# Recurrence kernel: the state's update issued ahead of VectorE's diagonal, the scatters one step later

## The chip, the cores and the metric

The kernel runs on one core of a Trainium2 chip. The metric is the device time of one execution in microseconds (us), from runs on the chip. All rows below are from one profiled execution.

## The reference

Three layers in a row on float32 data: a linear recurrence over 768 steps of time (4 batches, 8 heads, width 48), a layer of 8 experts in which each token goes to its best one, and a layer of 8 experts with 4 slots each that all tokens share. The change touches the first:

```
state = 0
for t in range(S):
    cur = u * k[t] (outer) v[t]
    y[t] = r[t] @ (state + cur)
    state = w * state + k[t] (outer) v[t]
```

The second layer takes y as rows x of 3072 tokens by 384: a token is computed if `x @ w_skip > 0`, and goes to the expert with the largest `x @ w_gate`. The third mixes all rows by two softmaxes.

## The kernel before

Time is cut into 6 chunks of 128; a chunk of one batch is one step of the loop at line 973, so 24 steps, step i with chunk `c = i // 4` and batch `b = i % 4`. Within a chunk the recurrence is done by matrix products: all pairs of times in the chunk give scores, which a mask and the powers of w weigh; the state carries what came before the chunk.

The order of the work is written out by hand: `manual_schedule` keeps every engine in the order in which the code emits its instructions, and waits between engines come from the buffers that the instructions read and write. What a step i emits, with its names:

- `load(i + 3)` (line 498): SyncE fetches r and k (`rkb`, two transfers) and k, v by rows (`kvt`), three steps ahead, with five buffers of each.
- `scores(i)` (626): TensorE makes the scores `sc` (line 633, two banks of PSUM, one buffer) from the scaled `rks`, and `dt` (636) from `pd`; ScalarE copies `dt` to `dts` (638).
- `inter(i - 1)` (694), `stateb(i - 1)` (670) and `trx(i - 2)` (717): the state's part of y, the copy of the state for it, and the turn of y into rows of x.
- `bonus(i)` (651): TensorE turns `dts` into the front columns of the tile `ud` (line 656), one bank of PSUM, of which there is one buffer. It holds the u term for the scores' diagonal.
- `prep(i + 1)` and `prepk(i + 1)` (611, 620): VectorE scales the next inputs to `rks` (616); GpSimd makes `pd` (618) and `kt` (624), which the next step's update needs.
- `amask(i)` (683): VectorE masks the scores into `at` (line 681) and puts the diagonal into them (688), read from the front columns of `ud`.
- `upd(i)` (640): TensorE makes the chunk's contribution to the state, eight products (line 649), into columns 160 to 351 of the same `ud`. Steps 20 to 23 have none.
- `state(i)` (658): GpSimd decays the old state to `tmp` (667), VectorE adds `ud` to it (668).
- `av(i - 1)` (704): TensorE's products of `at` and v into `yp` (712), copied out by ScalarE (715).

Every fourth step also routes the chunk before, in groups of four batches: `route1` (TensorE, 744) in one step; `route2` (TensorE, 804) and `route2b` (VectorE, 820 to 837) in the next; two steps on `route3` (TensorE, 847 to 856, into further columns of `ud`), `gates`, `places` and `count` (VectorE, 861 to 888, which also write the indices `idx`) and `route4` (GpSimd 903, ScalarE 905 and 907). With the indices there, `scat(j)` (890) has GpSimd write the rows of x of step j to their experts' slots by an indirect transfer (891): from step 8 on one in each step, the rest after the loop. In steps 8, 11 and 14 `wload` (912) fetches expert weights.

The dependencies are kept by bank of PSUM: two instructions of different engines that touch the same bank are put in the order of the code, even where their columns differ.

Of the kernel before, what the change touches and what calls it, by code (L numbers as in the profile page):

```python
# [461 lines left out]
def tile_main(ctx, tc, rk, kv, wu, wcat, phi, w1, w2, v1, v2, r_in, k_in, v_in, w_in, u_in, wcn, out, dbg=None, force=False):  # L462
# [177 lines left out]
    def upd(j):  # L640
        t = T[j]
        if j < NT - B:
            kt, kvt = t["kt"], t["kv"]
            up = t["up"] = t["ud"][0:PR, 160:352].rearrange("d (p e) -> d p e", p=4)
            for p in range(4):
                for hf in range(2):
                    h = 2 * p + hf
                    m = 64 if hf == 0 else D
                    nc.tensor.matmul(up[64 * hf : 64 * hf + m, p, :], kt[:, h * D : h * D + m], kvt[:, 1, h * D : h * D + D], start=True, stop=True)  # L649
# [28 lines left out]
    def past(j):  # L678
        t = T[j]
        at = t["at"] = wk.tile([P, 2, 4, P], F32, tag="at", name=f"at{j}")  # L680
        nc.vector.tensor_mul(at, t["sc"], mask.rearrange("s (a o t) -> s a o t", a=1, o=1).to_broadcast([P, 2, 4, P]))  # L681

    def amask(j):
        t = T[j]
        if "at" not in t:
            past(j)
        at = t["at"]
        nc.vector.copy_predicated(  # L688
            at,
            ident_i.rearrange("s (a o t) -> s a o t", a=1, o=1).to_broadcast([P, 2, 4, P]),  # L690
            t["dtk"].rearrange("s (p o r) -> s r p o", o=1, r=32)[:, 0:2].to_broadcast([P, 2, 4, P]),
        )
# [279 lines left out]
    if True:  # L972
        for i in range(NT):
            if i + 3 < NT:
                load(i + 3)
            rc, rb = divmod(i - 5, B)
            rok = 0 <= rc < NC_ - 1
            if i == 0:
                prep(0)
                for hf in range(2):  # L980
                    r0 = 64 * hf
                    nc.vector.tensor_copy(usel[r0 : r0 + D, :, hf : hf + 1], wt[r0 : r0 + D, 1, :].rearrange("p (a o) -> p a o", o=1))
            scores(i)
            if i > 0:
                inter(i - 1)
                stateb(i - 1)
            if i > 1:
                trx(i - 2)
            bonus(i)
            if i == 0:  # L990
                decays()
                warm(ps, "y", 7)
                prep(1)
                prepk(0)
                prepk(1)
                for b in range(B):
                    nc.gpsimd.memset(sbd[b], 0.0)
            elif i + 1 < NT:
                prep(i + 1)
                prepk(i + 1)  # L1000
            if rok and rb == 1:
                route2(rc)
            if rok and (rb == 3 or i == 23):
                route3(rc, place=T[i]["dk"][:, P:])
            if i == 22:
                mrt = rows(nc, cn, "t", rt, pa, "u", mcs[:, 0:1])
                nc.vector.tensor_copy(lx[:, 0:1, :], mrt)
            amask(i)
            upd(i)
            state(i)  # L1010
            if i > 0:
                av(i - 1)
            if rok and rb == 0:
                route1(rc)
            if i == 23:
                route1(5)
            if rok and rb == 1:
                route2b(rc)
            if i == 23:
                weave("gpgpgp", g=gates(4), p=places(4))  # L1020
            if rok and rb == 3:
                weave("gpgpgp", g=gates(rc), p=places(rc))
                count(rc)
                route4(rc)
            if i == 21:
                nc.vector.tensor_reduce(cmax, ltm[:, 0:16, :].rearrange("t b s -> t s b"), axis=AX.X, op=ALU.max)
                colmax(nc, cn, "t", pa, "u", mcs[:, 0:1], fourfold(nc, "t", rt, cmax))
            if i == 22:
                nc.vector.tensor_sub(ltm[:, 0:16, :], ltm[:, 0:16, :], lx[:, 0:1, :].to_broadcast([P, 16, 32]))
                nc.scalar.activation(ltm[:, 0:16, :], ltm[:, 0:16, :], AF.Exp)  # L1030
            if i in (8, 11, 14):
                wload((i - 8) // 3)
            if i == 2:
                nc.sync.dma_start(out=xs_d.rearrange("(a p) n -> p a n", p=P), in_=zt.rearrange("p (o n) -> p o n", o=1).to_broadcast([P, NSLOT // P, XW]))
            if 3 <= i < 7:
                constants(i)
            if i == 4:
                nc.gpsimd.tensor_copy(x[:, :, DM + 2 : DM + 3].bitcast(I32), row_i.rearrange("p (j o) -> p j o", o=1))
            if i == 6:
                wok = rt.tile([PR, 4], F32, tag="wok", name="wok")  # L1040
                nc.vector.tensor_scalar(wok, wt[:, 0, :], WLO, None, op0=ALU.is_ge)
                wok2 = rt.tile([PR, 4], F32, tag="wok", name="wok2")
                nc.vector.scalar_tensor_tensor(wok2, wt[:, 0, :], WHI, wok, op0=ALU.is_le, op1=ALU.mult)
                wmn = mk.tile([PR, 1], BF16, name="wmn")
                nc.vector.tensor_reduce(wmn, wok2, axis=AX.X, op=ALU.min)
            if 8 <= i < 24:
                scat(i - 8)
        for j in range(16, 20):
            scat(j)
        inter(23)  # L1050
        route2(5)
        direct(6, "ud")
        route2b(5)
        av(23)
        route3(5, "t", (4,))
        weave("ccgcpgcpgcpcc", c=choose(6, "lg"), g=gates(5), p=places(5))
        for j in range(20, 22):
            scat(j)
        scst.close()
        qst = ExitStack()  # L1060
        pr = qst.enter_context(tc.tile_pool(name="pr", bufs=1, space=PSUM, side="right"))
        pc = Banks(tp=[(pr, "tp", 2)], ds=[(pr, "ds", 1)])
        w1g = Weighted(nc, "t", pc, "ds", mk, ltm, 16, lambda j: x[:, j, 0 : DM + 1])
        trx(22, "tp", pc)
        direct(7, "y")
        route3(6, "ud", (4, 5))
        trx(23, "tp", pc)
        weave("gggccpcpcpccc", c=choose(7, "lgp"), g=gates(6), p=places(6))
        nc.scalar.copy(RT[7]["lg"], RT[7]["lgp"][:, :, 0:42])
        scat(22)  # L1070
        ap.close()
        xq = fst.enter_context(tc.tile_pool(name="xq", bufs=1))
        hst = ExitStack()
        hl = fst.enter_context(tc.tile_pool(name="hl", bufs=1))
        cw = hst.enter_context(tc.tile_pool(name="cw", bufs=2))
        route3(7, "t", (4, 5, 6))
        weave("gggppp", g=gates(7), p=places(7))
        scat(23)
        early = [(nm, n, split(nm, n, False)) for n in (0, 1) for nm in "ab"]
        nc.vector.scalar_tensor_tensor(ltm[:, 16:24, :], m8.to_broadcast([P, 8, 32]), NEG, lg8[:, :, 9:41], op0=ALU.mult, op1=ALU.add)  # L1080
        nc.vector.tensor_reduce(cmax2, ltm[:, 16:24, :].rearrange("t b s -> t s b"), axis=AX.X, op=ALU.max)
        nc.gpsimd.tensor_copy(lt[:, 16:24, :], lg8[:, :, 9:41])
        gv = Group("v", cmax2, ltm[:, 16:24, :], 8, lambda j: x[:, 16 + j, 0 : DM + 1], lx[:, 1:2, :], mcs[:, 1:2])
        gv.first()
        lows(*early[0])
        w1g.some(12)
        gv.second()
        DS = {"t": w1g.done()}
        lows(*early[1])
        gv.rows()  # L1090
        nc.vector.tensor_copy(gv.mrow, gv.mrp)
        nc.vector.tensor_sub(gv.lg, gv.lg, gv.mrow.to_broadcast([P, gv.nt, 32]))
        nc.scalar.activation(gv.lg, gv.lg, AF.Exp)
        for i in (2, 3):
            lows(*early[i])

        cntp = pc.tile([P, E + 1], F32, tag="tp", name="cntp")
        nc.tensor.matmul(cntp[:, 0:E], ones, ohacc, start=True, stop=False)
        for b in range(8):
            nc.tensor.matmul(cntp[:, 0:E], ones, oh8[:, b, :], start=False, stop=(b == 7))  # L1100
        nc.tensor.matmul(cntp[:, E : E + 1], ones[:PR, :], wmn, start=True, stop=True)
        cnt = mk.tile([P, E + 1, 1], F32, name="cnt")
        nc.vector.tensor_copy(cnt.rearrange("p e o -> p (e o)"), cntp)
        rst.close()
        pst.close()
        pl = qst.enter_context(tc.tile_pool(name="pl", bufs=1, space=PSUM))
        pc = Banks(tp=[(pr, "tp", 2)], ds=[(pr, "ds", 1)], hp=[(pl, "hp", 3)], y0=[(pr, "y0", 1)], y1=[(pl, "y1", 1)])
# [426 lines left out]
```

## Time and profile before

| what | us |
|---|---|
| runs shown (3) | 398.83, 402.29, 412.5 |
| their median | 402.29 |
| profiled execution | 398.23 |
| its span, first to last instruction | 396.5 |
| recurrence, scores of step 0 to those of step 23 | about 8 to 162 |
| experts and third layer | about 200 to 385 |

The profiled execution's time is taken from outside, the span from its first to its last instruction; 1.7 us lie around the span. Times in rows count from the span's start. Engines: PE is TensorE's products, PEld its weight loads, DVE VectorE, ACT ScalarE, POOL GpSimd, SP SyncE, which issues transfers. An idle time in brackets at a row's end stands for the time that the engine waited before it, with what released it; "issue" is time in which it waited for nothing that the profile shows.

### The profile page before, as it was taken

To read this page: it belongs to the slowest core of one execution; us is meant where nothing else is said; L and a number is where in the kernel's file an instruction comes from. 1 tells how busy PE (TensorE), PEld (TensorE's weight loads), DVE (VectorE), ACT (ScalarE), POOL (GpSimd) and SP (SyncE) were. 2 spreads that over 40 slices of the span, in tenths; PEclk is the share of its full clock that TensorE was granted. 3 is DMA by queue.
4 is the path that set the end of the run, shared out by engine and by line. 5 is a ranking of instruction groups with operands and counts; after the bars stand their busy time and mean duration, and the time that the engine had idled before them with its cause. 6 is when DMAs were issued, how large, how long until landed. Compare 5 with 4: busy or idle time off the path is not lost. (4 is left out here: it accounts for less than half of the span.)

```text
span 396.5 us, 8413 instructions
## 1 busy us (share of the span) xinstructions
PE 343.7 (87%) x3313; PEld 282.3 (71%) x3313; DVE 253.5 (64%) x496; ACT 161.6 (41%) x357; POOL 119.1 (30%) x149
## 2 busy tenths in 40 slices
PE   8678758776878879799999999999999999999960
PEld 3456557566667666665999999999989999853350
DVE  7877576576475579676684857585748584514760
ACT  1142324334323334353555555555546554311260
POOL 7843432854643816065001211111102010130000
PEclk9999989999886999999999999999999999999995
DMA  7999938777762440015997787787895664939676
GB/s 187 250 303 227 207 84 241 188 238 183 247 168 85 129 119 31 11 62 160 344 348 261 255 282 255 273 250 275 251 321 188 200 220 150 314 91 401 230 279 205
DMA packets 45696, 84.36 MB, mean 213 GB/s; under 512 B 3961, under 2 KB 26831, under 8 KB 45648
## 3 DMA queue, kind: packets, MB, share of 16 engines
q1 hardware_dynamic: 42320, 78.29, 63.5%
q0 software_dynamic: 2800, 5.28, 4.5%
q8 instruction: 28, 0.46, 0.5%
q10 hardware_dynamic: 528, 0.16, 0.2%
q14 instruction: 20, 0.16, 0.1%
HBM read 72.94 MB, written 13.30 MB: 217 GB/s over the span
## 5 line engine op out<-in xcount | busy, mean ns | idle before, releaser
L1140 PE MATMUL hp<-xhl,wa 128*128 128x256 f32 x192 | 48.6, 290 | 0.2 <-ACT xhl L1130 0.2
L1141 PE MATMUL hp<-xhl,wa 128*128 128x256 f32 x192 | 47.2, 282 | 0.0
L1165 PE MATMUL yp<-wb,hh 128*128 128x384 f32 x128 | 45.3, 354 | 0.0
L953 DVE TENSOR_TENSOR wa<-w,wa 128x768 fp32r<-128x768 f32 x32 | 30.6, 955 | 22.1 <-ACT wa L965 20.9
L1166 PE MATMUL yp<-wb,hh 128*128 128x384 f32 x128 | 43.1, 337 | 0.0
L1167 PE MATMUL yp<-wb,hlo 128*128 128x384 f32 x128 | 43.1, 337 | 0.0
L649 PE MATMUL ud<-kvt,kt 128*48 128x48 f32 (+1 forms) x320 | 13.9, 228 | 32.7 <-issue 23.7
L1198 POOL DMA_INDIRECT lt_d<-lsr,id x16 | 17.6, 1097 | 80.1 <-ACT xhl L1130 56.6
L681 DVE TENSOR_TENSOR at<-sc,mask 128x1024 f32<-128x1024 f32 x24 | 29.3, 1221 | 14.7 <-PE sc L633 14.7
L688 DVE COPY_PREDICATED at<-ident,ud 128x1024 f32<-128x1024 int32 x24 | 31.1, 1296 | 11.7 <-PE ud L856 5.6
L891 POOL DMA_INDIRECT xs_d<-x,idx x24 | 24.2, 1007 | 47.9 <-PE sc L633 13.5
L649 PEld LDWEIGHTS ud<-kvt,kt 128*48 128x48 f32 (+1 forms) x320 | 11.8, 140 | 36.7 <-issue 26.1
L715 ACT COPY yt<-yp 112x512 f32<-112x512 f32 x24 | 14.1, 586 | 57.6 <-PE yp L712 57.6
L1140 PEld LDWEIGHTS hp<-xhl,wa 128*128 128x128 f32 x192 | 36.3, 189 | 0.5 <-ACT xhl L1130 0.5
L1141 PEld LDWEIGHTS hp<-xhl,wa 128*128 128x128 f32 x192 | 36.5, 190 | 0.0
L618 POOL TENSOR_TENSOR pd<-rkb 112x512 f32<-112x512 f32 x24 | 30.8, 1282 | 17.3 <-PE dt L636 6.9
L953 DVE TENSOR_TENSOR wb<-w,wb 128x768 fp32r<-128x768 f32 x32 | 30.5, 955 | 3.1 <-ACT wb L965 3.1
L965 ACT CAST wb<-w 128x768 fp32r<-128x768 f32 x32 | 26.8, 837 | 9.0 <-PE yp L1167 5.0
L1151 DVE SCALAR_TENSOR_TENSOR hlo<-hp,hh 128x512 fp32r<-128x512 f32 x32 | 22.0, 688 | 12.4 <-ACT hh L1150 12.4
L1150 ACT ACTIVATE hh<-hp 128x512 fp32r<-128x512 f32 x32 | 19.2, 598 | 26.2 <-PE hp L1143 26.2
L633 PEld LDWEIGHTS sc<-rks 48*128 48x128 f32 x384 | 24.1, 193 | 7.9 <-issue 6.7
L616 DVE TENSOR_TENSOR rks<-rkb,prk 112x1024 f32<-112x1024 f32 x24 | 29.1, 1214 | 0.8 <-DMA rkb<-in_rk_dram 0.8
(330 smaller groups left out, 743.5 us busy)
## 6 DMA issues: line engine op xcount, KB each, us to landing
w<-in_w_dram SPq DMA_DIRECT2D x32, 768.0 KB, 5.7
v<-in_v_dram SPq DMA_DIRECT2D x29, 768.0 KB, 6.7
rkb<-in_rk_dram SPq DMA_DIRECT2D x48, 192.0 KB, 6.9
kvt<-in_kv_dram SPq DMA_DIRECT2D x24, 384.0 KB, 4.9
out_dram<-ob SPq DMA_DIRECT2D x5, 768.0 KB, 5.3
xs_d<-zt SPq DMA_DIRECT2D x1, 3096.0 KB, 14.6
xg<-xs_d POOLq DMA_DIRECT2D x6, 387.0 KB, 4.6
x<-in_v_dram SPq DMA_DIRECT2D x2, 768.0 KB, 7.0
```

The costliest lines, as they stand in the source:

```text
L616: nc.vector.tensor_mul(rks, rkt, prk)
L618: nc.gpsimd.tensor_mul(t["pd"], rkt[:, 0], rkt[:, 1])
L649: nc.tensor.matmul(up[64 * hf : 64 * hf + m, p, :], kt[:, h * D : h * D + m], kvt[:, 1, h * D : h * D + D], start=True, stop=True)
L681: nc.vector.tensor_mul(at, t["sc"], mask.rearrange("s (a o t) -> s a o t", a=1, o=1).to_broadcast([P, 2, 4, P]))
L688: nc.vector.copy_predicated(at, ident_i.rearrange("s (a o t) -> s a o t", a=1, o=1).to_broadcast([P, 2, 4, P]), t["dtk"].rearrange("s (p o ...
L953: nc.vector.tensor_sub(lv, sl, hv.bitcast(F32))
L965: nc.scalar.copy(hv, sl)
L1140: nc.tensor.matmul(hp[:, f, :], hi[:, k, fs], xh[:, k, :], start=(k == 0 and f == 0), stop=False)
L1141: nc.tensor.matmul(hp[:, f, :], lo[:, k, fs], xh[:, k, :], start=False, stop=False)
L1165: nc.tensor.matmul(YP[e][bl], hh[:, f, bs], hi[:, f, :], start=st, stop=False)
L1166: nc.tensor.matmul(YP[e][bl], hh[:, f, bs], lo[:, f, :], start=False, stop=False)
L1167: nc.tensor.matmul(YP[e][bl], hlo[:, f, bs], hi[:, f, :], start=False, stop=en)
```

## The change

The call of the update is put one line up, ahead of the diagonal, and the scatters begin in step 9 instead of 8:

```
             if i == 22:
                 mrt = rows(nc, cn, "t", rt, pa, "u", mcs[:, 0:1])
                 nc.vector.tensor_copy(lx[:, 0:1, :], mrt)
+            upd(i)
             amask(i)
-            upd(i)
             state(i)
             if i > 0:
                 av(i - 1)
...
-            if 8 <= i < 24:
-                scat(i - 8)
-        for j in range(16, 20):
+            if i > 8:
+                scat(i - 9)
+        for j in range(15, 20):
             scat(j)
```

On TensorE and VectorE the instructions keep their order; their waits change. Here is TensorE in step 9 before, from the bonus to the scores of step 10 (`ud9` is the shared tile, `kt9` and `kvt9` the update's inputs):

```order
L656 MATMUL ud9_883<-ident_126,dts9_868 128x128 [waits DVE_49]
L649 MATMUL ud9_883<-kvt9_603,kt9_796 64x48 [waits DMAHW1_49,DVE_49,Pool_49]
L649 MATMUL ud9_883<-kvt9_603,kt9_796 48x48
L712 MATMUL yp8_870<-at8_804,kvt8_529 48x128 x8
L744 MATMUL lgt1_915<-yt1_590,wcs_118 64x512 x4
L633 MATMUL sc10_929<-rks10_885 128x128 x8
```

And the same place now:

```order
L656 MATMUL ud9_880<-ident_126,dts9_865 128x128 [waits DVE_49]
L649 MATMUL ud9_880<-kvt9_603,kt9_796 64x48 [waits DMAHW1_49,Pool_49]
L649 MATMUL ud9_880<-kvt9_603,kt9_796 48x48
L712 MATMUL yp8_867<-at8_812,kvt8_529 48x128 x8
L744 MATMUL lgt1_912<-yt1_590,wcs_118 64x512 [waits DVE_49]
L633 MATMUL sc10_926<-rks10_882 128x128 [waits DVE_49]
```

The update's wait on VectorE is gone, those on its load and on GpSimd stay; the router products and the next scores, which came after it, have waits on VectorE of their own. VectorE in step 9, before:

```order
L616 TENSOR_TENSOR rks10_885<-rkb0_106,prk_184 112x1024 [waits DMAHW3_49,DMAHW2_49]
L681 TENSOR_TENSOR at9_891<-sc9_854,mask_136 128x1024 [waits PE_49]
L688 COPY_PREDICATED at9_891<-ident_126,ud9_883 128x1024 [waits DVE_49,PE_49]
L668 TENSOR_TENSOR sp1_189<-ud9_883,tmp9_902 112x192 [waits PE_49,Pool_49]
L616 TENSOR_TENSOR rks11_960<-rkb1_107,prk_184 112x1024 [waits DMAHW6_49,DMAHW5_49]
```

And now:

```order
L616 TENSOR_TENSOR rks10_882<-rkb0_106,prk_184 112x1024 [waits DMAHW3_49,DMAHW2_49]
L681 TENSOR_TENSOR at9_896<-sc9_851,mask_136 128x1024 [waits PE_49]
L688 COPY_PREDICATED at9_896<-ident_126,ud9_880 128x1024 [waits DVE_49,PE_49]
L668 TENSOR_TENSOR sp1_189<-ud9_880,tmp9_899 112x192 [waits Pool_49]
L616 TENSOR_TENSOR rks11_957<-rkb1_107,prk_184 112x1024 [waits DMAHW6_49,DMAHW5_49]
```

The state (668) waits for TensorE no more: the diagonal (688) ahead of it now waits for the update, where it waited for the bonus. GpSimd at the end of step 8, which routes a group, before (`pd10` and `kt10` are made for step 10, `xs_d` is what a scatter writes):

```order
L903 COPY ltt_162<-lg0_647 128x128 [waits DVE_49]
L891 DMA xs_d_124<-x_159,idx_165 2048x387 [waits DVE_49,Activation_49]
L618 TENSOR_TENSOR pd10_887<-rkb0_106 112x512 [waits DMAHW2_49,DMAHW3_49,PE_49,Pool_49]
L624 TENSOR_TENSOR kt10_889<-kvt10_695,pktok_187 128x384 [waits DMAHW4_49,PE_49,Pool_49]
L667 TENSOR_TENSOR tmp9_902<-sp1_189,pt_172 112x192 [waits Pool_49]
```

And now:

```order
L903 COPY ltt_162<-lg0_647 128x128 [waits DVE_49]
L618 TENSOR_TENSOR pd10_884<-rkb0_106 112x512 [waits DMAHW2_49,DMAHW3_49,PE_49,Pool_49]
L624 TENSOR_TENSOR kt10_886<-kvt10_695,pktok_187 128x384 [waits DMAHW4_49,PE_49,Pool_49]
L667 TENSOR_TENSOR tmp9_899<-sp1_189,pt_172 112x192 [waits DVE_49]
L891 DMA xs_d_124<-x_159,idx_165 2048x387 [waits DVE_49,Activation_49]
```

The first scatter of a group, which waits for the indices that VectorE writes in this step, has moved behind the three products of the next step.

## Rows read from the trace of the kernel before

**Rows 1.** Busy time by stretch: length, engines with their instructions, granted clock, DMA share, GB/s
```profile
47.00:145.00 98.00, 74.38 (x987) 60.96 (x987) 64.34 (x116) 34.04 (x94) 48.37 (x55) 0.91 0.62 171
...
200.00:385.00 185.00, 182.45 (x1386) 157.84 (x1384) 115.39 (x217) 90.75 (x179) 24.55 (x31) 1.00 0.75 253
```
**Rows 2.** Order of events, step 12: start, length, engine, line, operands, idle time before
```profile
87.04 1.16 PE L633 MATMUL sc<-rks 48*128 48x128 f32 x16
...
89.84 0.27 PE L656 MATMUL ud<-ident,dts 128*128 128x128 f32 x1
...
90.29 1.29 DVE L688 COPY_PREDICATED at<-ident,ud 128x1024 f32<-128x1024 int32 x1 [0.81 <-PE ud L856]
...
91.68 0.58 PE L649 MATMUL ud<-kvt,kt 128*64 128x48 f32 x15 [1.43 <-issue]
92.08 0.28 PE L712 MATMUL yp<-at,kvt 128*48 128x128 f32 x1
...
92.44 0.36 DVE L668 TENSOR_TENSOR sp<-ud,tmp 112x192 f32<-112x192 f32 x1 [0.86 <-PE ud L649]
...
93.12 1.16 PE L633 MATMUL sc<-rks 48*128 48x128 f32 x16
```
**Rows 3.** Order of events, TensorE, scores of steps 20 and 21
```profile
145.61 1.16 PE L633 MATMUL sc<-rks 48*128 48x128 f32 x16
...
149.76 1.16 PE L633 MATMUL sc<-rks 48*128 48x128 f32 x16
```
**Rows 4.** Order of events, TensorE, router products of step 5, scores and transposes of step 6
```profile
42.66 0.32 PEld L744 LDWEIGHTS lgt<-yt,wcs 112*64 112x64 f32 x4
...
44.65 1.16 PE L633 MATMUL sc<-rks 48*128 48x128 f32 x16
...
47.44 0.47 PEld L804 LDWEIGHTS lgp<-ident,lgs 128*128 128x128 f32 x4
```
**Rows 5.** Order of events, VectorE's routing in steps 6 and 12, ScalarE behind it
```profile
50.21 0.32 DVE L820 TENSOR_TENSOR lg<-lg,lgp 128x168 f32<-128x168 f32 x1
...
52.01 0.36 DVE L566 TENSOR_REDUCE sel<-ident 128x32 f32<-128x128 f32 x1
...
53.91 1.22 DVE L616 TENSOR_TENSOR rks<-rkb,prk 112x1024 f32<-112x1024 f32 x1
...
93.96 1.22 DVE L616 TENSOR_TENSOR rks<-rkb,prk 112x1024 f32<-112x1024 f32 x1
94.08 0.17 ACT L905 ACTIVATE mn<-lgp 128x4 f32<-128x4 f32 x1 [0.25 <-DVE ohacc L888]
...
95.15 0.24 ACT L638 COPY dts<-dt 128x128 f32<-128x128 f32 x1
```
**Rows 6.** Order of events, GpSimd's scatters of steps 9, 10 and 12
```profile
71.98 1.03 POOL L891 DMA_INDIRECT xs_d<-x,idx  x1 [0.16 <-issue]
...
75.91 1.00 POOL L891 DMA_INDIRECT xs_d<-x,idx  x1 [0.17 <-issue]
...
94.36 1.01 POOL L891 DMA_INDIRECT xs_d<-x,idx  x1 [6.26 <-PE sc L633]
```
**Rows 7.** Order of events, GpSimd's first product for step 6, VectorE's mask of step 5
```profile
37.00 1.28 POOL L618 TENSOR_TENSOR pd<-rkb 112x512 f32<-112x512 f32 x1 [4.44 <-DMA rkb<-in_rk_dram]
...
38.20 1.22 DVE L681 TENSOR_TENSOR at<-sc,mask 128x1024 f32<-128x1024 f32 x1
```
**Rows 8.** Scores of step 16 in the order of events; busy time of 116 to 118 us
```profile
115.42 2.08 PE L633 MATMUL sc<-rks 48*128 48x128 f32 x16
...
116.00:118.00 2.00, 2.00 (x24) 1.41 (x20) 0.52 (x2) 0.13 (x1) 0.33 (x2) 0.50 0.63 195
```
**Rows 9.** Order of events, VectorE and GpSimd side by side, steps 6 and 9
```profile
52.35 1.25 DVE L1041 TENSOR_SCALAR wok<-wt 112x4 f32<-112x4 f32 x1
...
69.10 1.30 POOL L618 TENSOR_TENSOR pd<-rkb 112x512 f32<-112x512 f32 x1
...
69.83 1.30 DVE L688 COPY_PREDICATED at<-ident,ud 128x1024 f32<-128x1024 int32 x1
```

More of the change, by code (lines that the diff above doesn't have):

```diff
@@ L1007, in tile_main @@
                 nc.vector.tensor_copy(lx[:, 0:1, :], mrt)
+            upd(i)
             amask(i)
-            upd(i)
             state(i)
@@ L1045, in tile_main @@
                 nc.vector.tensor_reduce(wmn, wok2, axis=AX.X, op=ALU.min)
-            if 8 <= i < 24:
-                scat(i - 8)
-        for j in range(16, 20):
+            if i > 8:
+                scat(i - 9)
+        for j in range(15, 20):
             scat(j)
```

## The prediction

> **What bounds the kernel now.** I read the busy time by stretch first. In the recurrence from 47 to 145 us TensorE is busy 74.38 of 98 us, VectorE 64.34, GpSimd 48.37, the DMA engines 0.62 of the time [rows 1]: nothing is full, so waits set the pace. The page's chain of waits is no help, since it holds one branch at the end of the program; the order of events in one step tells what sets the pace. From here on steps are counted as the loop counts them (i), and "scores" are line 633, "bonus" line 656, "update" line 649, "diagonal" line 688, "state" line 668.
>
> Step 12 [rows 2]: the scores start at 87.04, the bonus at 89.84, VectorE's diagonal at 90.29. The diagonal takes 1.29 us, and only then, at 91.68, does TensorE issue the update, after an idle stretch of 1.43 us. The profile names no releaser ("issue"), but the update starts 0.10 us after the diagonal's end, and the order shows the wait on VectorE. Behind the update stand on TensorE the attention product of step 11 (line 712, at 92.08) and the scores of step 13 (93.12). So the step takes 6.08 us: 2.80 from scores to bonus, 1.84 from bonus to update, 1.44 from update to the next scores. VectorE in its turn waits 0.86 us behind the diagonal until the update is done and starts the state at 92.44. Each engine waits for the other within one step.
>
> Step 20 has no update (only steps 0 to 19 have), and so no wait on the diagonal: from its scores at 145.61 to the next at 149.76 are 4.15 us [rows 3]. With the update's own 0.40 us (91.68 to 92.08, [rows 2]) that makes 4.55, against the 6.08 of step 12; both steps hold the same extra, six small products of the routing.
>
> **The change part by part.** The instructions are the same on every engine; on TensorE and VectorE even their order is. What changes is which wait stands where. The update no longer waits for VectorE, and the diagonal waits for the update instead of the state. The scores of the next step now carry a wait of their own, for the masked scores (line 681), which read the same buffer.
>
> *A plain step* then takes on TensorE 2.80 (scores to bonus) + about 0.10 (bonus to update, the gap between two products that wait for nothing, my estimate) + 1.44 = 4.35 us. Three times in four a step holds more: 2.0 us of router products (42.66 to 44.65), 0.47 us of transposes [rows 4], and 0.24 us of small products, from 4.55 less 4.35, rounded up. Four steps: 4 x 4.35 + 2.0 + 0.47 + 0.24 = 20.1 us.
>
> *VectorE.* The diagonal now begins 0.76 us after the update's start (91.68 to 92.44 was that latency for the state), so at 2.80 + 0.10 + 0.76 = 3.66 us after the scores of its step; before it was 3.25 in step 12. That later start is hidden as long as VectorE has time: per step it needs 1.22 (scaling, line 616, [rows 5]) + 1.22 (mask, line 681, [rows 7]) + 1.29 (diagonal) + 0.36 (state) = 4.09 us, four steps 16.4. The routing adds 1.80 in one step of four (50.21 to 52.01) and 1.16 in another (from the state at 92.44 to the next scaling at 93.96, less the state's 0.36) [rows 2, 5]: 19.4 us. This is under 20.1, but it is not evenly spread. Behind the first routing the next mask ends at 3.66 + 0.47 + 1.29 + 0.36 + 1.80 + 1.22 + 1.22 = 10.0 us after the scores of the routing's step, while TensorE would have the scores after next at 4.35 + 0.47 + 4.35 = 9.2: 0.8 us late. Behind the second, ScalarE is in the way: line 905 waits for the last routing operation, and only 1.07 us after its start (94.08 to 95.15, [rows 5]) comes the copy on which the next bonus waits. The diagonal there begins at 3.66 + 0.24, so that copy ends at 3.90 + 1.29 + 0.36 + 1.16 + 0.12 + 1.07 + 0.24 = 8.1, and with about 0.7 for the transposes between (an estimate from the 2.80) the bonus comes at 8.8 instead of 4.35 + 0.24 + 2.80 = 7.4: 1.4 us late. So 20.1 + 0.8 + 1.4 = 22.3, with a little for gaps 22.4 us for four steps.
>
> *GpSimd.* Its product for the update (line 624) is now what the update, the diagonal and all behind them wait for. A round of scatter, two products and state term takes 3.93 us (71.98 to 75.91, [rows 6]), four 16.0 with a small copy, under 22.4. In the kernel before the first scatter of a group stood ahead of these products and waited 6.26 us for its indices (the row names the scores; by the order the wait is on VectorE, which writes the indices); moved one step later it waits behind the products of the step. The sixteenth scatter, now issued after the loop instead of in it, costs 1.0 us where GpSimd otherwise has nothing to do until the next indices; without that cover it would cost those 1.0 us. I put the scatter part at nothing by itself: it keeps the first part from being eaten up.
>
> *The start.* Up to step 5 the loads decide, not the engines: GpSimd's first product of step 6 waits 4.44 us for its load until 37.00, and VectorE's scaling of step 6 needs the same load; the mask of step 5 follows it at 38.20 [rows 7]. A faster chain can't bring that forward. But TensorE then has all of step 5 behind it, router products included, and the scores of step 6 wait only for that mask: 38.20 + 1.22 + 0.1 = 39.5 instead of 44.65 [rows 4]. Gain 5.1 us.
>
> *The sum.* From the scores of step 6 to those of step 20 it was 145.61 - 44.65 = 100.96 us. Now: three groups of four at 22.4 (67.2), steps 18 and 19 (2 x 4.35 + 0.47 = 9.2), and 1.90 us of constants that VectorE makes once in step 6 (52.01 to 53.91, [rows 5]): 78.3 us. Gain 22.7, all at the full clock. In the kernel before the clock was not always full: at 116 to 118 us the granted clock is 0.50, that is 1.2 GHz, and the scores of that step took 2.08 us [rows 8] where those of step 12 took 1.16. Over 47 to 145 us the mean is 0.91 [rows 1], so at most 0.09 x 98 = 8.8 us were lost; part of that lay beside waits. I take 6 as lost before and half of it, 3 us, as lost again, since TensorE will still idle now and then. Sum: 5.1 + 22.7 - 3.0 = 24.8 us. Nothing behind step 20 changes: the experts run TensorE 182.45 of 185 us [rows 1], so the gain carries through. The profiled execution took 398.23 us (span 396.5): 398.2 - 24.8 = 373.4. The runs shown lie higher, from 398.83, with a median of 402.29, 1% above. I forecast 375 us for a typical run.
>
> **The rivals.** *Loads (0.10).* From 47 to 145 us transfers fill 0.62 of 98 us, 60.8 us that must now fit into about 78. On the mean they do; but three times a pair of expert weights (1.5 MB; at 171 / 0.62 = 276 GB/s 5.6 us, [rows 1]) stands ahead of the next step's inputs. Against it: inputs are issued about three steps ahead, some 14 us. A third of the 17 us exposed gives 381, all of it 392.
>
> *GpSimd late (0.06).* If its product keeps coming as late as behind the waiting scatter, each of the 3.5 groups loses about 3 us again: 10 us, so 385. For it: a round fills 3.93 of a 4.35 us step. Against: buffers of two let it run ahead, and the scatter's wait is gone.
>
> *The low clock stays or goes (0.15 and 0.12).* If all of it stays, 378; if it vanishes and VectorE's late steps are hidden too (3.5 x 2.3 = 8 us, half of it), 367.
>
> *No gain (0.04).* If the update waits for GpSimd as long as it waited for the diagonal, the change does not do what it says: 398 to 402.
>
> *Slower (0.04).* The diagonal, now packed more closely beside GpSimd's products, is held up by them. Line 1041, a VectorE operation on four columns, took 1.25 us [rows 9], about what a GpSimd product takes; I count 1.1 us of it as blocking by such a product. Twice a step, on scaling and diagonal, over 20 steps that is 44 us, so 375 + 44 = 419; it decides against the change from 1.2 us per step on, and shows as slower by 2% from 1.6. Against it: in step 9 the diagonal (69.83) ran beside GpSimd's product (69.10 to 70.40) and took 1.30 us [rows 9], against 1.29 in step 12, so I give this case little. The Trainium skill has the rule (SBUF — State Buffer, section "SBUF: two separate sides"): VectorE and GpSimd share one pair of ports as an exclusive lock, and whoever starts first holds it for the whole instruction, where VectorE runs in a two-port mode or has two SBUF inputs. By that rule line 1041 is explained and the trace agrees there; the diagonal's row does not show it.
>
> **How the numbers follow.** The forecast (370 to 380) holds 0.49; with loads 0.10, GpSimd 0.06, clock staying 0.15, clock gone 0.12, no gain 0.04, slower 0.04 that is all. The range 365 to 388 leaves out no gain, slower, and the far half of the loads. About 2%, 8 us, is what a measurement of this kernel tells from no change: faster by more 0.88, within it 0.08 (no gain, and the far end of the loads), slower 0.04.
>
> **What would show it right or wrong.** Right: the idle time of TensorE ahead of the update gone or put down to GpSimd; the diagonal waiting for line 649; steps of 4.4 to 4.8 us with no routing in them; scores of step 6 near 39.5 and of step 20 near 117 to 121; ScalarE's line 905 just ahead of a late bonus. Wrong: updates that wait 1 us or more for line 624; diagonals or scalings over 1.4 us; waits of lines 616 or 624 on DMA behind the weight loads; a granted clock under 0.9 from 40 to 120 us.

## The result, and the profile after

The changed kernel takes **377.19 us** (median of 4 runs, 373.98 to 377.54); the kernel before, beside it, 403.16 (398.83 to 412.5). The ratio is **0.937, 95% interval 0.927 to 0.947**: faster by 6%. The ratio leaves out the run of 412.5 us, over 1.5% above the fastest of its kernel. The forecast was 375 us, the range 365 to 388. The profiled execution has a span of 375.4 us, 21.1 less than before. The head of its page:

```profile
span 375.4 us, 8403 instructions
PE 344.7 (92%) x3313; PEld 280.3 (75%) x3313; DVE 250.4 (67%) x496; ACT 160.6 (43%) x357; POOL 118.8 (32%) x149
PEclk9999989999999998589999999999999999999995
```

TensorE's busy time hardly moved; its share rose because the span shrank around it. The clock's row has two dips besides its last slice, which is low in both kernels: a small one in the sixth slice, a deep one in slices 16 to 18. The first is in the recurrence, the second behind it, where the prediction had seen nothing change.

**One step.** Step 12 in the order of events, first TensorE, then VectorE, against [rows 2]:

```profile
72.19 1.16 PE L633 MATMUL sc<-rks 48*128 48x128 f32 x16 [0.38 <-DVE at L681]
...
75.10 0.27 PE L656 MATMUL ud<-ident,dts 128*128 128x128 f32 x1
...
75.45 0.61 PE L649 MATMUL ud<-kvt,kt 128*64 128x48 f32 x15
...
75.95 1.04 PE L712 MATMUL yp<-at,kvt 128*48 128x128 f32 x15
...
76.92 1.16 PE L633 MATMUL sc<-rks 48*128 48x128 f32 x16
...
76.17 1.32 DVE L688 COPY_PREDICATED at<-ident,ud 128x1024 f32<-128x1024 int32 x1
...
77.38 0.34 DVE L668 TENSOR_TENSOR sp<-ud,tmp 112x192 f32<-112x192 f32 x1
```

The update follows the bonus after 0.35 us (six small products lie between), where it took 1.84. The idle 1.43 us ahead of it are gone, and the step takes 4.73 us instead of 6.08. The diagonal starts 3.98 us after the scores instead of 3.25, and the state now follows it without a wait. Scores of a step can wait for a mask (0.38 us at 72.19), as foreseen.

**Where the 21.1 us came from.** All times in the first three columns are read from the order of events, scores of a step to scores of another; "experts" is their first product (line 1140).

| stretch | before | forecast | after | gain |
|---|---|---|---|---|
| start to scores of step 6 | 44.65 | 39.5 | 37.33 | 7.3 |
| step 6 to step 20 | 100.96 | 78.3, and 3 of low clock | 79.31 | 21.7 |
| step 20 to step 23 | 16.73 | unchanged | 17.33 | -0.6 |
| step 23 to experts | 23.42 | unchanged | 30.54 | -7.1 |
| experts to the end of the span | 210.7 | unchanged | 210.9 | -0.2 |

Three groups of four steps (6 to 18) took 25.03, 21.84 and 21.84 us; before it was 29.75, 28.23 and 30.34. Not all of that is the change: in before_again (below) the second group ran at the full clock and took 26.58 us. At the full clock a group so gains 4.7 us; the other 1.7 and 3.8 us of the second and third group are, by that figure, low clock in the profiled execution of the kernel before.

**The start.** TensorE's scores of step 6, VectorE's two operations that they hang on, and the issue of the 3 MB of zeros in step 2:

```profile
37.33 1.16 PE L633 MATMUL sc<-rks 48*128 48x128 f32 x16 [1.59 <-DVE at L681]
...
34.92 1.22 DVE L616 TENSOR_TENSOR rks<-rkb,prk 112x1024 f32<-112x1024 f32 x1 [4.17 <-DMA rkb<-in_rk_dram]
36.05 1.22 DVE L681 TENSOR_TENSOR at<-sc,mask 128x1024 f32<-128x1024 f32 x1
...
17.28 0.43 SPq L1034 DMA_DIRECT2D xs_d<-zt  x1
```

And the zeros in the kernel before:

```profile
20.57 0.43 SPq L1034 DMA_DIRECT2D xs_d<-zt  x1
```

The chain is the forecast one (load, scaling, mask of step 5, scores of step 6), but the load came at 34.92 and not at 37.00 [rows 7]. The zeros ahead of it in the queue went out at 17.28; in the kernel before SyncE issued them at 20.57, behind a load that waits for a buffer, and buffers now come free earlier: from 8 to 40 us SyncE's loads of line 505 waited 12.1 us in all for TensorE's line 712, which reads the buffer, and now 3.6.

**ScalarE and GpSimd behind the second routing** (step 13), against [rows 5, 6]:

```profile
79.00 0.17 ACT L905 ACTIVATE mn<-lgp 128x4 f32<-128x4 f32 x1 [1.37 <-DVE ohacc L888]
79.21 0.96 ACT L907 ACTIVATE ltt<-lg,mn 128x32 f32<-128x32 f32 x4
80.07 0.24 ACT L638 COPY dts<-dt 128x128 f32<-128x128 f32 x1
...
80.37 0.60 PE L721 MATMUL trp<-ident,yt 112*128 112x112 f32 x4 [0.87 <-ACT dts L638]
80.81 0.27 PE L656 MATMUL ud<-ident,dts 128*128 128x128 f32 x1
...
79.29 0.99 POOL L891 DMA_INDIRECT xs_d<-x,idx  x1 [1.54 <-ACT mn L905]
```

The bonus comes 3.89 us after the scores (76.92) instead of 2.91 in step 12: line 905 stands ahead of the copy that it needs. The first scatter of a group waits 1.54 us instead of 6.26.

**Busy time** of the recurrence and of the experts, against [rows 1], and the diagonals over the whole program, against [rows 9]:

```profile
47.00:125.00 78.00, 70.62 (x978) 57.29 (x978) 64.10 (x113) 33.55 (x96) 47.41 (x54) 0.98 0.77 210
180.00:365.00 185.00, 181.28 (x1379) 156.65 (x1377) 114.12 (x214) 89.77 (x177) 24.47 (x31) 1.00 0.74 252
...
L688 DVE COPY_PREDICATED at<-ident,ud 128x1024 f32<-128x1024 int32 x24 | 31.6, 1315 | 12.1 <-PE ud L649 6.9
```

TensorE is busy 0.91 of the recurrence (0.76 before), the clock is 0.98 (0.91), transfers fill 0.77 (0.62). The diagonal takes 1.315 us in the mean.

**Behind the recurrence.** Busy time from 135 to 165 us, then ScalarE, VectorE, TensorE and GpSimd at 147 us:

```profile
135.00:140.00 5.00, 3.32 (x41) 2.80 (x39) 4.16 (x12) 1.49 (x4) 0.00 (x0) 0.89 0.00 0
140.00:145.00 5.00, 5.00 (x44) 3.92 (x42) 1.81 (x13) 1.48 (x5) 2.62 (x3) 0.77 0.10 36
145.00:150.00 5.00, 3.15 (x46) 2.76 (x41) 2.66 (x24) 1.21 (x4) 2.19 (x3) 0.91 0.13 46
150.00:155.00 5.00, 4.85 (x37) 1.57 (x35) 2.58 (x15) 3.71 (x7) 2.27 (x4) 0.50 0.17 61
155.00:160.00 5.00, 4.06 (x26) 1.73 (x26) 4.25 (x10) 0.90 (x2) 1.83 (x3) 0.50 0.31 96
160.00:165.00 5.00, 4.76 (x30) 1.82 (x28) 1.41 (x4) 1.40 (x4) 1.50 (x3) 0.72 0.90 261
...
147.61 0.58 ACT L715 COPY yt<-yp 112x512 f32<-112x512 f32 x1 [2.57 <-PE trp L721]
147.71 0.17 DVE L872 TENSOR_TENSOR r<-rp,oh 128x16 f32<-128x16 f32 x1 [1.86 <-PE trp L721]
148.25 1.14 PE L764 MATMUL lgp<-wcs,yt 112*128 112x42 f32 x8 [1.85 <-ACT yt L715]
149.13 0.98 POOL L891 DMA_INDIRECT xs_d<-x,idx  x1 [2.51 <-ACT x L722]
```

ScalarE and VectorE both wait for TensorE, whose records end at 146.4, and are released 1.2 us later; TensorE then waits for ScalarE, and GpSimd for ScalarE's copy of x (line 722). ScalarE reads only what line 712 made, and the last record of that line ends 1.9 us before the release (144.59 + 1.08 = 145.67):

```profile
144.59 1.08 PE L712 MATMUL yp<-at,kvt 128*48 128x128 f32 x16
```

From 150 to 160 us the granted clock is 0.50, that is 1.2 GHz. In the kernel before, the same operations of TensorE, ScalarE and VectorE came without such a wait, and the clock there was under 1 only from 175 to 180 us (0.66):

```profile
171.35 1.08 PE L712 MATMUL yp<-at,kvt 128*48 128x128 f32 x16
172.48 0.59 ACT L715 COPY yt<-yp 112x512 f32<-112x512 f32 x1 [0.60 <-PE yp L712]
172.76 0.17 DVE L872 TENSOR_TENSOR r<-rp,oh 128x16 f32<-128x16 f32 x1
173.12 1.09 PE L764 MATMUL lgp<-wcs,yt 112*128 112x42 f32 x8
```

### The profile page after: what moved, and what is told of

It reads as the page before. It is cut to its first block, busy times and chain, and to the rows that moved or that the text cites. A ratio compares the mean times of both kernels' runs of the same rounds, so it can differ in the third digit from the quotient of the medians.

```text
span 375.4 us, 8403 instructions
## 1 busy us (share of the span) xinstructions
PE 344.7 (92%) x3313; PEld 280.3 (75%) x3313; DVE 250.4 (67%) x496; ACT 160.6 (43%) x357; POOL 118.8 (32%) x149
## 5 line engine op out<-in xcount | busy, mean ns | idle before, releaser
L1140 PE MATMUL hp<-xhl,wa 128*128 128x256 f32 x192 | 48.6, 290 | 0.2 <-ACT xhl L1130 0.2
L1141 PE MATMUL hp<-xhl,wa 128*128 128x256 f32 x192 | 47.2, 282 | 0.0
L688 DVE COPY_PREDICATED at<-ident,ud 128x1024 f32<-128x1024 int32 x24 | 31.6, 1315 | 12.1 <-PE ud L649 6.9
L618 POOL TENSOR_TENSOR pd<-rkb 112x512 f32<-112x512 f32 x24 | 30.6, 1277 | 24.8 <-DMA rkb<-in_rk_dram 10.1
L633 PEld LDWEIGHTS sc<-rks 48*128 48x128 f32 x384 | 23.3, 187 | 13.0 <-DVE at L681 7.9
L633 PE MATMUL sc<-rks 48*128 48x128 f32 x384 | 27.9, 285 | 5.5 <-DVE at L681 5.4
L616 DVE TENSOR_TENSOR rks<-rkb,prk 112x1024 f32<-112x1024 f32 x24 | 29.1, 1213 | 5.2 <-DMA rkb<-in_rk_dram 4.9
L1143 PE MATMUL hp<-xhl,wa 128*128 128x256 f32 x192 | 28.3, 283 | 0.0
L712 PE MATMUL yp<-at,kvt 128*48 128x128 f32 (+1 forms) x384 | 28.0, 281 | 0.0
```

The source lines that it names most:

```text
L616: nc.vector.tensor_mul(rks, rkt, prk)
L618: nc.gpsimd.tensor_mul(t["pd"], rkt[:, 0], rkt[:, 1])
L633: nc.tensor.matmul(sc[:, hf, p, :], ks[r0 : r0 + D, p, :], rs[r0 : r0 + D, p, :], start=True, stop=True)
L688: nc.vector.copy_predicated(at, ident_i.rearrange("s (a o t) -> s a o t", a=1, o=1).to_broadcast([P, 2, 4, P]), t["dtk"].rearrange("s (p o ...
L1140: nc.tensor.matmul(hp[:, f, :], hi[:, k, fs], xh[:, k, :], start=(k == 0 and f == 0), stop=False)
L1141: nc.tensor.matmul(hp[:, f, :], lo[:, k, fs], xh[:, k, :], start=False, stop=False)
```

## The experiments

The table gives for each the median, the ratio to the kernel before beside it with its interval, the three groups of four steps (scores 6 to 10, 10 to 14, 14 to 18), and the stretch from the scores of step 23 to the experts. The kernel before is another set of runs from row to row: its median was 399.56 us beside the first four rows, 400.26 beside exp_behind_bonus, fill_in_pieces and all_four, and 402.58 beside the last two variants and after_again. Medians of different rows can differ for that reason too; by the ratios, masks_behind_bonus, constants_in_load_wait and exp_behind_bonus can't be told from the changed kernel (0.937 and 0.938), so what they did is read from the stretches. The profile of four_without_the_change is of an execution of 407.3 us, and no stretches are read from it.

| run | median us | ratio | groups us | 23 to experts |
|---|---|---|---|---|
| update_first_only | 375.82 | 0.941 (0.932 to 0.949) | 24.85, 22.26, 21.91 | 27.73 |
| scatter_later_only | 402.21 | 1.008 (1.004 to 1.012) | 30.05, 26.58, 28.11 | 30.51 |
| masks_behind_bonus | 372.68 | 0.935 (0.926 to 0.944) | 23.05, 20.74, 20.74 | 28.19 |
| constants_in_load_wait | 375.10 | 0.936 (0.927 to 0.945) | 23.38, 21.87, 21.83 | 30.54 |
| exp_behind_bonus | 371.39 | 0.936 (0.928 to 0.944) | 24.91, 21.82, 21.80 | 23.15 |
| fill_in_pieces | 366.19 | 0.922 (0.914 to 0.929) | 23.94, 21.82, 21.81 | 23.48 |
| all_four | 363.81 | 0.916 (0.908 to 0.925) | 20.62, 20.63, 20.62 | 23.92 |
| all_four_scatters_early | 365.77 | 0.912 (0.903 to 0.921) | 20.62, 20.62, 20.63 | 26.46 |
| four_without_the_change | 402.23 | 0.999 (0.994 to 1.004) | - | - |
| after_again | 375.78 | 0.938 (0.929 to 0.948) | 25.29, 21.82, 21.80 | 27.67 |
| before_again | 396.86 (one run) | none | 30.10, 26.58, 28.20 | 24.53 |

**Which part of the change does it?** The update alone, written as an edit of the changed kernel (the scatters go back):

```diff
-            if i > 8:
-                scat(i - 9)
-        for j in range(15, 20):
+            if 8 <= i < 24:
+                scat(i - 8)
+        for j in range(16, 20):
```

> The update moved ahead of the diagonal, the scatters left where they were before the change. If the second part of the change protects the first (my theory): GpSimd holds the first scatter of a group in front of its next three products until the indices of that group are written, some 6 us, so its four rounds (16.0 us) and that wait make 22.2 us per group, just over the 21.84 us that a group of four steps takes in the changed kernel; with a product that comes late now and then 0.5 to 3 us are lost per group, in all 379 to 387 us. If the scatters' place is worth nothing (rival): 375 to 378.5 us and groups of 21.8 us.

375.82 us: the rival's figure. The first scatter of a group does wait, and the whole group still fits:

```profile
79.73 1.00 POOL L891 DMA_INDIRECT xs_d<-x,idx  x1 [6.26 <-DMA rkb<-in_rk_dram]
83.64 1.01 POOL L891 DMA_INDIRECT xs_d<-x,idx  x1 [0.17 <-ACT yt L715]
...
101.64 1.00 POOL L891 DMA_INDIRECT xs_d<-x,idx  x1 [6.24 <-ACT mn L905]
```

A group takes 101.64 - 79.73 = 21.91 us on GpSimd, 6.24 of them waiting; the products behind the scatter are ready before TensorE wants them: from 37 to 120 us TensorE waits for GpSimd nowhere. The scatters alone (the opposite edit, on the kernel before):

> The order of update and diagonal as before the change, only the scatters one step later. My theory: nothing, since each step then waits for the diagonal and not for GpSimd; 0.99 to 1.01 of the kernel before, four-step groups of 28 to 30 us. Rival, that GpSimd's wait also cost time in the kernel before: 1 to 3 us per group, 388 to 395 us.

1.008 of the kernel before: no gain, rather a loss of 0.4 to 1.2%. Its recurrence is as fast as that of before_again (97.38 and 97.52 us from step 6 to step 20), but from step 23 to the experts it takes 30.51 us instead of 24.53. So the first part of the change makes the whole gain, and the second adds nothing that these runs show.

To see whether the scatters' place matters once everything else is shorter, they were put back in the kernel with all four edits (below):

> The kernel with four edits, the scatters put back to where they were before the change. With the update alone moved, GpSimd had to wait 6.2 us per group in front of its products, and its 16.0 us of work and that wait make 22.2 us; groups took 22.26 and 21.91 us there, little over the 21.84 that ScalarE and TensorE set. If that sum is right: with the others gone, groups go from 20.6 back to 21.9 to 22.3 us, and the time is 4 to 6 us over the 363.8 of the kernel with four edits: 368 to 370 us. Rival, the scatters' place never matters: 362 to 365 us, groups of 20.6.

Groups stayed at 20.62, and the sum that my theory rested on is refuted by the row of the wait itself:

```profile
73.45 1.00 POOL L891 DMA_INDIRECT xs_d<-x,idx  x1 [4.66 <-DMA rkb<-in_rk_dram]
...
94.07 1.00 POOL L891 DMA_INDIRECT xs_d<-x,idx  x1 [4.94 <-ACT dts L638]
```

The wait shrank from 6.2 to 4.7 to 4.9 us as the group got shorter: it is what is left of the period after GpSimd's 16 us, not a cost to be added to them. The time, 365.77 us, is 2 us over all_four's, less than the 4 to 6 us of the theory, and the stretch from step 23 on is 2.5 us longer there.

**ScalarE ahead of the bonus.** The mask operations of lines 905 and 907 are kept in a list and issued behind the next step's bonus:

```diff
             bonus(i)
+            masks()
```

> The changed kernel, with ScalarE's five mask operations of the routing moved from the end of their step to behind the next step's bonus. My theory: in the changed kernel the copy ahead of the bonus waits for them once per group, and the bonus comes 3.89 us after the scores instead of 2.80, in steps 9, 13, 17 and 21; that goes, groups of four steps take 20.7 to 21.0 us instead of 21.84, in all 372 to 374 us for the 377 of the changed kernel. Rival, VectorE (19.4 us of work per group, unevenly spread) is the limit behind ScalarE: the next scores wait longer for the mask instead, groups stay at 21.5 to 21.9 and the time at 376 to 378.

Groups of 20.74 us, 1.10 less than the 21.84 of the changed kernel, as the theory had it, and 372.68 us. In the same step 13 the bonus now comes 2.79 us after the scores:

```profile
75.87 1.16 PE L633 MATMUL sc<-rks 48*128 48x128 f32 x16
...
78.66 0.27 PE L656 MATMUL ud<-ident,dts 128*128 128x128 f32 x1
```

**The constants of step 6** (lines 566, 567 and 1041 to 1045) moved into VectorE's wait for the load, ahead of the scaling of step 6:

```diff
             elif i + 1 < NT:
+                if i == 5:
+                    constants(6)
...
                 prep(i + 1)
```

> The changed kernel, with VectorE's five operations on constants of step 6 moved ahead of the scaling of step 6, where it waits 4.17 us for a load. My theory: the scores of step 8 come 1.5 us earlier (they wait 2.05 us for the mask in the changed kernel), and if the low clock that follows that wait goes too, another 1.4 us: 374 to 376 us. Rival, the scores of step 8 are held by the late load of step 6 and not by the constants: they start where they did, 377 us.

From the scores of step 6 to those of step 10 it is 23.38 us instead of 25.03, 1.65 less, about the constants' own time. But the scores of step 8 didn't come 1.5 us earlier: they start at 49.43, where it was 48.92, and their distance from the scores of step 6 shrank by 0.2 us only. The low clock didn't go, it moved to step 6 (a granted clock of 0.76 from 38 to 45 us); the end of the program took its 30.54 us again, and the time is 375.1.

**The exponential of step 22** (line 1030) behind the bonus of step 23:

```diff
-                nc.scalar.activation(ltm[:, 0:16, :], ltm[:, 0:16, :], AF.Exp)
...
             bonus(i)
+            if i == 23:
+                nc.scalar.activation(ltm[:, 0:16, :], ltm[:, 0:16, :], AF.Exp)
```

> The changed kernel, with ScalarE's exponential of step 22 (line 1030) moved behind the bonus of step 23. My theory: the bonus of step 23 no longer waits 1.68 us for the copy that stands behind the exponential; VectorE's diagonal there comes 0.7 us earlier, and the stretch from the scores of step 23 to the experts gets 0.7 to 1.7 us shorter, 375.5 to 376.5 us. If the low clock that follows the wait in the changed kernel goes with it, 2 us more. Rival: something else ends last there, and nothing changes, 377 us.

371.39 us, a lower time than either case gave. TensorE's transposes of step 23 no longer wait:

```profile
133.75 1.16 PE L633 MATMUL sc<-rks 48*128 48x128 f32 x16 [0.40 <-DVE at L681]
...
136.17 0.60 PE L721 MATMUL trp<-ident,yt 112*128 112x112 f32 x4
```

The standstill 12 us after the scores of step 23 was absent too, and the granted clock stayed at 1.00 from 130 to 155 us: 23.15 us for the stretch. The next run shows that the standstill can also be absent without this edit.

**The zeros in six pieces.** The one transfer of step 2 (line 1034) is cut over steps 2 to 7:

```diff
-            if i == 2:
+            if 2 <= i < 8:
+                na = NSLOT // P
+                a0, a1 = na * (i - 2) // 6, na * (i - 1) // 6
```

> The changed kernel, with the 3.2 MB of zeros that are written to memory in step 2 cut in six pieces over steps 2 to 7. My theory, as in the prediction: up to step 6 the loads decide; the input of step 6 stands behind the zeros in the queue and lands some 8 us earlier without them, VectorE's wait of 4.17 us ahead of its scaling goes, and the scores of step 6 start at 33.5 to 35 us instead of 37.33: 373.5 to 375.5 us. Rival, transfers are full up to step 9 whatever their order: the scores of step 10 start where they did, 62.4 us, and the time stays at 377.

366.19 us. The scores of step 6 start at 35.66, not at 33.5 to 35, and no load holds them:

```profile
30.69 1.21 DVE L616 TENSOR_TENSOR rks<-rkb,prk 112x1024 f32<-112x1024 f32 x1
...
33.77 1.96 PE L744 MATMUL lgt<-yt,wcs 112*64 112x512 f32 x8
35.66 1.16 PE L633 MATMUL sc<-rks 48*128 48x128 f32 x16
```

The scaling of step 6 comes at 30.69 without a wait (34.92 before the edit), and TensorE runs through step 5 with its router products to the scores of step 6; I had left those 2.0 us out. That part is worth 37.33 - 35.66 = 1.7 us. But 7.1 us of the gain lie where the edit changes nothing: from step 23 to the experts it took 23.48 us instead of 30.54, with the 1.67 us wait of the transposes still there. So the loss at the end comes and goes with edits that do not touch it.

**The loss at the end, again.** The two kernels once more:

> The kernel before, once more. From the scores of step 23 to the first product of the experts it took 23.42 us in the profiled execution; the changed kernel took 30.54 there and four variants 27.7 to 30.5, with a granted clock under 1 in part of it and, 12 us behind the scores of step 23, a wait of about 1.9 us of TensorE for ScalarE's copy in line 715. If the 23.42 was luck of that one execution (my theory): 27 to 31 us here, with that wait. If the change itself lengthens this stretch (rival): 23 to 24 us again, and the change gives some 6 us of its gain back there.

> The changed kernel once more. Theory: the stretch from the scores of step 23 to the experts is longer in it by the same few us each time (27 to 31 us, with a wait of about 1.9 us for line 715 and a granted clock under 1 behind it), since four other kernels show it with little change; 374 to 378 us. Rival, it comes and goes by execution: 23 to 25 us in this one, and some of the times near 370.

24.53 and 27.67 us: in the kernel before nearly the rival's figure, in the changed one the theory's. The kernel before was short there twice, the changed one long twice, with the wait of TensorE for line 715 both times (1.85 and 2.02 us). The same wait is in update_first_only, scatter_later_only, masks_behind_bonus and constants_in_load_wait (1.9 to 2.5 us), and not in exp_behind_bonus, fill_in_pieces or all_four. So it goes with the kernel rather than with chance, as far as two profiles each of two kernels can tell, and also with one whose recurrence is as slow as before (scatter_later_only, 30.51 us). The stretch falls into three parts, cut at the last products of line 712 (144.59 and 171.35 above) and at the products of line 764 behind them (148.25; 173.12 before):

| part of the stretch, us | before | before_again | after | after_again |
|---|---|---|---|---|
| scores of step 23 to line 712 | 9.01 | 10.57 | 10.62 | 10.58 |
| line 712 to line 764 | 1.77 | 1.77 | 3.66 | 3.82 |
| line 764 to the experts | 12.64 | 12.19 | 16.26 | 13.27 |

Of the 7.1 us, 1.9 are the standstill. Ahead of it 1.6 are lost in a stretch of low clock (0.50 from 138.9 to 142.3 us) that before_again has too, without a standstill. The other 3.6 lie behind it, with the clock of 0.50; in after_again they are 0.6. What makes the standstill stays open.

**All four edits together**, and the same four without the change:

> The changed kernel with four edits: ScalarE's masks behind the bonus, the constants in the load's wait, the exponential behind the bonus of step 23, the zeros in six pieces. If the gains add up (1.1 us per group, 1.5, about 1 and about 3 us): 366 to 369 us, groups of 20.7 us. If VectorE or the transfers become the limit when the others are gone: 370 to 373 us.

> The same four edits on the kernel before, without the change (update behind the diagonal, scatters at their old place). Theory: the wait of TensorE and VectorE for each other sets the pace of steps 6 to 19, groups stay at 25.5 to 27 us at the full clock; the masks on ScalarE gain at most 1 us per group, the constants 1.5 us, the zeros little, since steps of 5.7 us wait less for loads: 385 to 393 us, so the change is still worth 22 to 29 us on top. Rival, the change and the edits are worth something only one by one (the same bound): under 375 us.

With the change: 363.81 us, 12 to 13 less than the medians of the changed kernel (ratio 0.916 against 0.937 and 0.938, intervals that don't overlap), less than the 366 to 369 to which the single gains were added up, and with the one that differs only in the scatters the best here. A group (56.29 to 76.92 us) is now full on TensorE, 20.25 of 20.63 us at full clock:

```profile
56.29:76.92 20.63, 20.25 (x296) 16.57 (x295) 18.01 (x33) 9.96 (x28) 15.54 (x18) 1.00 0.99 268
```

Without it the same edits are worth nothing (ratio 0.999), less than either case had it. The wait of TensorE behind the diagonal is still there in step 12, 1.43 us as in [rows 2]:

```profile
89.82 0.58 PE L649 MATMUL ud<-kvt,kt 128*64 128x48 f32 x15 [1.43 <-issue]
```

Steps 10 to 13 take 5.95, 6.70, 6.08 and 9.52 us, in the kernel before 5.94, 6.70, 6.08 and 9.51. So in these steps TensorE and VectorE waiting for each other hid what the masks gain. That the same wait hid the other three edits isn't shown: at the end this kernel has a wait of 4.36 us where all_four_scatters_early has one of 4.37, and what was won elsewhere may have been given back there.

## Why the prediction was right, and where its steps were off

**What bounds the kernel: right, and shown.** The update alone gives 0.941, the whole change 0.937, with overlapping intervals; the scatters alone give nothing. The stall of 1.43 us went, and what would be late next was named rightly: a mask (0.38 us) and ScalarE's line 905.

**Four steps: 22.4 forecast, 21.84 measured.** The steps 10 to 13 took 4.91, 4.92, 4.73 and 7.28 us. Two terms were too large. "0.8 us late" behind the first routing is a wait of 0.38 us. "1.4 us late" behind the second is 3.89 - 2.91 = 0.98 in the row and 1.10 where masks_behind_bonus takes it away. Together they are 0.7 to 0.8 too large; the steps themselves were a little too small. A late mask was left out of the sum: steps 18 and 19 took 10.60 us (4.91 and 5.69) instead of 9.2. VectorE has the first routing in step 19 as in step 11, and the scores of step 20 wait 0.57 us for the mask.

**The start: 39.5 forecast, 37.33 measured.** The failing step is "A faster chain can't bring that forward". Loads wait for buffers, which the faster chain frees earlier: the zeros left 3.29 us earlier (20.57 to 17.28) and the load behind them landed 2.1 us earlier.

**GpSimd: the sum held, the meaning didn't.** 16 us of work per group left room, as said. But "it keeps the first part from being eaten up" is refuted twice, at groups of about 22 and of 20.6 us: the early scatter's wait shrinks with the room.

**The low clock: less in the recurrence, more behind it.** I took 3 us as lost again in the recurrence. There it was about 1.4: step 8 (scores at 48.92, the next at 55.08) took 6.16 us where step 12, which does the same work, took 4.73, with a granted clock of 0.64 from 49 to 53 us, behind a wait of 2.05 us for a mask.

```profile
48.92 1.16 PE L633 MATMUL sc<-rks 48*128 48x128 f32 x16 [2.05 <-DVE at L681]
...
49.00:53.00 4.00, 4.00 (x36) 3.53 (x37) 3.77 (x4) 0.66 (x3) 1.26 (x1) 0.64 1.02 307
```

**Behind step 20: the step that failed.** "Nothing behind step 20 changes" and "so the gain carries through": 7.7 us were given back there in the profiled run (0.6 to step 23, 7.1 to the experts: 1.6 of low clock, 1.9 of standstill, 3.6 behind it). Against before_again's 24.53 us, after_again's 27.67 give back 3.1. The start (2.2 us) and the recurrence (2.0 us) gained more than forecast, so that the sum, 24.8 us, missed the measured 21.1 by 3.7 only. The forecast came out near partly because these errors have opposite signs.

**The rivals.** Loads: transfers fill 0.77 of the recurrence and 0.99 in all_four, and groups are at TensorE's time all the same; not exposed. GpSimd late: refuted by update_first_only. No gain: refuted. Slower by blocking: the diagonals take 1.315 us in the mean where they took 1.296, 0.02 us each, and all scalings together 29.1 us in both kernels, far from the 1.2 us a step at which that rival decides. The lock between VectorE and GpSimd that the Trainium skill states (SBUF — State Buffer, "SBUF: two separate sides") can be behind no more than the 0.5 us by which all diagonals together grew (31.1 to 31.6). The diagonals before:

```profile
L688 DVE COPY_PREDICATED at<-ident,ud 128x1024 f32<-128x1024 int32 x24 | 31.1, 1296 | 11.7 <-PE ud L856 5.6
```

That line 1041 was held up before is borne out: it now starts at 46.04, as GpSimd's product ends, and takes 0.16 us instead of 1.25. The rival of the vanished clock adds up to 368 by its own terms (375 less 3 and 4), not 367; no chance or bound hangs on it.

**Open.** Why the results of TensorE reach two engines 1.2 us after its records end, in some kernels and not in others, isn't settled. The Trainium skill says (Perfetto Trace Analysis, "Tensor Engine Instruction (MATMUL, LD_WEIGHTS)") that the ends of matmuls in a trace are estimated, and that the release follows only when the writes are acknowledged; that allows a late release but doesn't say why it is late here. A fetch of instructions doesn't lie beside it: from 140 to 149 us the only transfers are those of the scatters. That the low clock behind the standstill (3.6 us here, 0.6 in after_again) follows from it wasn't tried.

## What to carry to other kernels

Where two engines each wait for the other once per step over one shared buffer, let the engine that everybody waits for go first, and look which small operation stands ahead of the next critical copy; here four edits elsewhere were worth nothing while that wait stood (0.999 without the change; with it from 0.937 on to 0.916). A wait in a profile is not work: before adding it to an engine's sum, ask whether it shrinks when the step gets shorter. A gain in one stage has to be followed to the end of the program: the stage behind it can give part of it back, and a variant's total says nothing of an edit until the stretches that the edit doesn't touch have been compared.

## What the runs showed that I had not expected

- The stretch from step 23 to the experts, the same instructions in nearly the same order, took between 23.15 and 30.54 us, and 30.54 to the hundredth in two different kernels.
- In all_four_scatters_early another such standstill lies one round of the routing's products later, and in four_without_the_change at the same place: TensorE waits 4.37 and 4.36 us for VectorE (line 795). In the first, TensorE's last record ends at 137.97, and VectorE and ScalarE are released at 141.18 and 141.36; the profile names none of the core's engines as releaser:

```profile
141.18 0.16 DVE L775 TENSOR_SCALAR m<-lgp 128x1 f32<-128x1 f32 x1 [3.59 <-remote]
```

- Cutting one transfer of 3 MB into six pieces took the load's wait of 4.17 us away, though the transfers' share up to 35 us stayed full (1.04).
